# Head outputs of a tile pair split over two PSUM banks by parity, and a last feed-forward step in two halves

## The chip, the cores and the metric

The kernel runs on one core of one Trainium2 chip, in float32 (matrix products of the feed-forward layers in fp32r with each operand split into a high and a low part). The metric is the device time of one execution in microseconds. Before the change three executions took 596.48, 597.11 and 599.32 us: median 597.11.

## The reference

A chunked linear attention ("scan"), whose output goes through two feed-forward layers. Sizes: batch 4, 8 heads, sequence 768, head size 32, state size 16; 3072 tokens of 256 features; hidden size 2048.

```python
for c in range(nc):                                   # per head, chunk of the sequence
    cum = np.cumsum(la, axis=-1)
    M = CB * exp(cum_i - cum_j) * causal              # CB = C_i . B_j
    y = M @ xc + (Cc @ state) * exp(cum)              # inside the chunk + carried state
    state = exp(sum(la)) * state + sum_j B_j x_j decay_from_j
x = y as (3072 tokens, 256)                           # head h gives features 32h..32h+31
h = x @ w_in;   x = np.maximum(0.01 * h, h) @ w_out   # layer 0
h = x @ w_in2;  out = (h * np.cos(h)) @ w_out2        # layer 1
```

## The kernel before

The 768 positions are cut into six blocks of 128, and a block of all four sequences (`NB`) is 4 x 128 = 512 tokens. Per block there is an attention stage and then layer 0 and layer 1; `JOBS` orders the twelve layer jobs (0 0 0 1 1 0 1 0 1 0 1 1), and the attention of block b + 1 runs beside layer 0 of block b.

Attention works on token tiles of 128 positions of one sequence (`TokenTile`, j = 0 to 3), each in two chunks s of 64. Per tile TensorE runs `cb` (scores, L467), `products` (L487: decayed scores times x for each head and chunk; L491: the state's contribution), and `carried` (L500: state times C). All are small matmuls on parts of the array: L467, L487 and L491 on 64 rows and 32 columns, L500 on 32 rows and 32 columns. The program writes each as one float32 matmul. VectorE multiplies scores by decays (`decay`, L475) and carries the state (L524). The outputs of head h = 2p + q stand on partitions 32p to 32p + 31, in columns 256 + 64q on, and `y_cols` says so. An even tile uses the tile `att` (two PSUM banks, one for each chunk s), an odd tile two one-bank tiles of tag `g`; `x_hi` (L511, ScalarE) and `x_lo` (L515, VectorE) copy them out as the high and low parts of the layer's input x1, one instruction each for an even tile, two for an odd one. Layer 1 uses the `g` banks for hidden tiles when no attention runs.

A layer job has 16 steps f of 128 hidden features: six input matmuls (L658 to L660) into `h` (or, in layer 1, for odd f, `g`), an activation chain (layer 0: L668; layer 1: L671 ScalarE, L674 VectorE, L679 ScalarE, L683 VectorE), a split into `hi` (L306 or L308) and `lo` (L314 or L316), and six output matmuls (L698 to L700) into two `y` banks. At the end of layer 1 the two `y` are copied (L754) and stored (L757). Layer 0 of block 0 runs its first three steps in halves of 256 tokens. Weights arrive as float64 bits and are rebuilt on ScalarE, VectorE and GpSimd (L306 to L359) during the first 120 us.

The order on each engine is written out ahead of time: `Order.run` is a list scheduler that takes each operation's engine costs (us), due time, reads and writes, and starts the ready operation with the earliest due time on each free engine. An operation can hold many instructions (all `carried` of a pair and the following `cb` are one). Between engines the instructions wait on semaphores. Until the first feed-forward matmul, spare warm-up matmuls (L265) fill free TensorE time; the first `WARM_FIRST` stand at the very start.

```python
def y_cols(self, h, s):
    p, q = divmod(h, 2)
    return bank(self.t, s)[32 * p:32 * p + 32, 256 + Q * q:256 + Q * q + Q]
```

## Time and profile before

| | |
|---|---|
| median of three executions | 597.11 us (596.48 to 599.32) |
| profiled execution | 598.55 us, of which span 596.7 us (first to last instruction) |
| TensorE matmul, weight load | 98%, 80% of the span busy; 5013 instructions each |
| VectorE, ScalarE, GpSimd | 55%, 59%, 46% busy |
| mean granted TensorE clock | 0.989 |
| chain that ended last | TensorE 94%, VectorE 2%, ScalarE 2%, issue 1%, DMA 1% |
| instruction queue q8 | 39 packets, 0.64 MB |

The span runs from the first to the last instruction. Engines work side by side, so an engine's busy time is of use only where that engine sets the pace. "Issue" stands for time in which an engine waited for nothing that the profile shows. A float32 matmul shows as two records of an instruction. In an ordered list, `[x <-Y]` says that the engine was idle for x us before the instruction and that Y ended it; equal neighbours are merged into one row with their count. The last number of a table of stretches' clock column is the share of full speed granted to TensorE.

### The profile page before, as it was taken

Reading aid. Unit: us, or ns where it says so; the run is one execution under the profiler, and the core shown is the slowest. Engines: PE = TensorE matmul, PEld = TensorE weight load, DVE = VectorE, ACT = ScalarE, POOL = GpSimd, SP = SyncE. Lnnn points to the kernel's source line nnn. Section 1 sums busy time; section 2 is a strip of 40 time slices with the busy share of each in tenths; the row PEclk is TensorE's granted clock in tenths of the full one; section 3 lists DMA queues with packets and bytes.
Section 4 is the critical chain, followed back from the end, with each engine's and each line's share of the span. In section 5 each row is a group of like instructions: output and inputs, shape, how many; then the busy total and the mean of one; then the engine's idle time right before and its main releaser. Section 6 shows DMA issues by size and latency. Waiting matters only on the chain.

```text
span 596.7 us, 12418 instructions
## 1 busy us (share of the span) xinstructions
PE 584.7 (98%) x5013; PEld 475.5 (80%) x5013; DVE 326.3 (55%) x615; ACT 350.7 (59%) x575; POOL 273.6 (46%) x231
## 2 busy tenths in 40 slices
PE   6899999999999999999999999999999999999996
PEld 4688878788788888888788888878888888888884
DVE  4789996684695665661273653120665002566654
ACT  3799957679766556555335554434755444655553
POOL 2212417449613446455445445543555444654441
PEclk9799999999999999999999999999999999999999
DMA  8597534643640001001150001000000100000101
GB/s 283 175 284 238 152 108 137 215 140 111 198 124 0 1 1 37 0 2 35 43 173 2 1 1 36 1 3 0 2 1 2 35 1 0 1 1 6 30 1 36
DMA packets 25497, 39.00 MB, mean 65 GB/s; under 512 B 2176, under 2 KB 8320, under 8 KB 25440
## 3 DMA queue, kind: packets, MB, share of 16 engines
q1 hardware_dynamic: 25440, 38.22, 20.3%
q8 instruction: 39, 0.64, 0.5%
q14 instruction: 18, 0.15, 0.1%
HBM read 34.96 MB, written 3.24 MB: 64 GB/s over the span
## 4 chain that ended last, share of the span: by engine, by line
PE 94%; DVE 2%; ACT 2%; issue 1%; DMA 1%; SPq 0%; DVEq 0%; ACTq 0%
PE y L698 15%; PE y L700 14%; PE y L699 14%; PE h L658 11%; PE h L659 11%; PE h L660 11%; PE g L658 4%; PE g L659 3%; PE g L660 3%; PE att L467 1%; PE g L467 1%; PE att L500 1%; PE g L500 1%; PE att L487 1%; PE g L487 1%
## 5 line engine op out<-in xcount | busy, mean ns | idle before, releaser
L314 POOL TENSOR_TENSOR lo<-u,hi 128x512 fp32r<-128x512 f32 x160 | 210.2, 1316 | 231.3 <-DVE hi L308 87.7
L668 ACT ACTIVATE u<-h 128x512 f32<-128x512 f32 (+1 forms) x99 | 58.6, 592 | 99.8 <-PE h L660 92.2
L679 ACT ACTIVATE k<-k,half_pi 128x512 f32<-128x512 f32 x96 | 69.5, 724 | 51.1 <-DVE k L674 50.6
L306 ACT ACTIVATE hi<-u 128x512 fp32r<-128x512 f32 (+1 forms) x119 | 74.4, 625 | 7.5 <-DVE u L683 2.5
L698 PE MATMUL y<-hi,wo0h 128*128 128x512 f32 (+1 forms) x198 | 78.3, 396 | 0.0
L658 PE MATMUL h<-x1h,wi0h 128*128 128x512 f32 (+1 forms) x198 | 77.2, 390 | 0.0
L659 PE MATMUL h<-x1l,wi0h 128*128 128x512 f32 (+1 forms) x198 | 76.4, 386 | 0.0
L660 PE MATMUL h<-x1h,wi0l 128*128 128x512 f32 (+1 forms) x198 | 76.4, 386 | 0.0
L700 PE MATMUL y<-lo,wo0h 128*128 128x512 f32 (+1 forms) x198 | 76.3, 385 | 0.0
L699 PE MATMUL y<-hi,wo0l 128*128 128x512 f32 (+1 forms) x198 | 76.2, 385 | 0.0
L698 PE MATMUL y<-hi,wo1h 128*128 128x512 f32 x192 | 74.9, 390 | 0.4 <-ACT hi L306 0.4
L700 PE MATMUL y<-lo,wo1h 128*128 128x512 f32 x192 | 75.0, 390 | 0.3 <-DVE lo L316 0.3
L699 PE MATMUL y<-hi,wo1l 128*128 128x512 f32 x192 | 74.8, 389 | 0.0
L674 DVE SCALAR_TENSOR_TENSOR k<-k,h 128x512 f32<-128x512 int32 x48 | 33.0, 688 | 71.4 <-ACT k L671 71.4
L683 DVE TENSOR_TENSOR u<-h,k 128x512 f32<-128x512 f32 x48 | 33.2, 692 | 37.1 <-ACT k L679 36.3
L683 DVE TENSOR_TENSOR u<-g,k 128x512 f32<-128x512 f32 x48 | 33.2, 692 | 34.3 <-ACT k L679 32.2
L671 ACT ACTIVATE k<-h 128x512 int32<-128x512 f32 x48 | 28.6, 597 | 30.3 <-PE h L660 30.1
L671 ACT ACTIVATE k<-g 128x512 int32<-128x512 f32 x48 | 28.7, 598 | 28.3 <-PE g L660 28.2
L698 PEld LDWEIGHTS y<-hi,wo0h 128*128 128x128 f32 x198 | 37.5, 189 | 9.5 <-issue 1.4
L658 PEld LDWEIGHTS h<-x1h,wi0h 128*128 128x128 f32 x198 | 37.6, 190 | 7.8
L700 PEld LDWEIGHTS y<-lo,wo0h 128*128 128x128 f32 x198 | 37.5, 189 | 7.8 <-DVE lo L316 0.4
L660 PEld LDWEIGHTS h<-x1h,wi0l 128*128 128x128 f32 x198 | 37.6, 190 | 7.6 <-DVE wi0l L316 0.2
(129 smaller groups left out, 1055.6 us busy)
## 6 DMA issues: line engine op xcount, KB each, us to landing
raw<-w_in SPq DMA_DIRECT2D x16, 512.0 KB, 3.8
head<-headp SPq DMA_DIRECT2D x24, 256.0 KB, 4.0
tok<-tokp SPq DMA_DIRECT2D x24, 256.0 KB, 4.1
abc<-a_clip SPq DMA_DIRECT2D x40, 128.0 KB, 3.9
raw<-w_out SPq DMA_DIRECT2D x8, 512.0 KB, 3.8
out_t<-u SPq DMA_DIRECT2D x12, 256.0 KB, 2.6
x2h<-w_out SPq DMA_DIRECT2D x4, 512.0 KB, 5.1
x2l<-w_out SPq DMA_DIRECT2D x4, 512.0 KB, 4.7
```

The source lines that it names most:

```text
L306: A.activation(out, in_, AF.Copy, scale=scale, bias=bias)
L314: G.tensor_tensor(out=out, in0=a, in1=b, op=op)
L658: PE.matmul(o, lhsT=wh, rhs=xh, start=(c == 0), stop=False)
L659: PE.matmul(o, lhsT=wh, rhs=xl, start=False, stop=False)
L660: PE.matmul(o, lhsT=wl, rhs=xh, start=False, stop=(c == 1))
L668: A.activation(make(u, "u", [128, n], F32)[:, 0:m], tiles[h][:, 0:m], AF.Prelu, alpha=0.01)
L671: A.activation(make(k, "k", [128, n], I32), tiles[h], AF.Copy, scale=INV2PI, bias=0.25)
L679: A.activation(t, t, AF.Sin, bias=half_pi)
L683: V.tensor_tensor(out=t, in0=tiles[h], in1=tiles[k].bitcast(F32), op=ALU.mult)
L698: PE.matmul(o, lhsT=wh, rhs=gh, start=(f == q.start == 0), stop=False, **skip)
L699: PE.matmul(o, lhsT=wl, rhs=gh, start=False, stop=False, **skip)
L700: PE.matmul(o, lhsT=wh, rhs=gl, start=False, stop=(f == KF - 1), **skip)
```

## The change

The heads are set in two lists: `OUT_HEADS[0]` = 0, 2, 4, 6 and `OUT_HEADS[1]` = 5, 7, 1, 3. Place u of list q goes to partitions 32u on. The outputs of both tiles of a pair (j = 0, 1 or 2, 3) stand together: list 0 in the even tile's two banks, list 1 in the odd tile's two; the columns are chosen by the parity of j. The features of x1 are so permuted, and `w_in`'s rows are permuted on the host to match. `products` and `carried` run over q, chunk and place in the new order; `out_of` copies the outputs of a pair (three instructions on ScalarE, three on VectorE) as one planned operation each. Block 0 works in pairs too, and its scores use 64 columns of the array at a time instead of 32. The warm-up matmuls are 512 wide instead of 256, and half as many.

In the last job the last step f = 15 runs in two halves of 256 tokens; the second half's hidden tile has the other tag. For f > 8 of that job the output matmuls are due 3.5 steps after the input matmuls instead of 2.5. Each `y` is copied in halves (first half on ScalarE, second on VectorE) and stored in halves.

```diff
-WARM = 300
-WARM_N = 256
-WARM_FIRST = 22
+WARM = 150
+WARM_N = 512
+WARM_FIRST = 11
+OUT_HEADS = [[2 * p for p in range(4)], [2 * ((p + 2) % 4) + 1 for p in range(4)]]
...
+            w = 64 if self.first else 32
             for r in range(2):
                 for g in range(2):
-                    for c in range(4):
-                        rows, i = slice(64 * g, 64 * g + 64), Q * (c // 2)
-                        PE.matmul(bank(t, g)[32 * c:32 * c + 32, 128 * r:128 * r + 128].rearrange("p (q i) -> p q i", q=2),
-                                  lhsT=k[rows, T * r + 32 * c:T * r + 32 * c + 32],
+                    for c in range(0, T, w):
+                        rows, i = slice(64 * g, 64 * g + 64), Q * (c // Q)
+                        PE.matmul(bank(t, g)[c:c + w, 128 * r:128 * r + 128].rearrange("p (q i) -> p q i", q=2),
+                                  lhsT=k[rows, T * r + c:T * r + c + w],
                                   rhs=k[rows, 2 * T:4 * T].rearrange("p (q i) -> p q i", q=2)[:, :, i:i + Q],
                                   start=(r == 0), stop=True, skip_group_check=True)
...
-        def y_cols(self, h, s):
-            p, q = divmod(h, 2)
-            return bank(self.t, s)[32 * p:32 * p + 32, 256 + Q * q:256 + Q * q + Q]
+        def y_cols(self, q, u, s):
+            c = 256 + Q * (self.j % 2)
+            return bank(self.t - self.t % 2 + q, s)[32 * u:32 * u + 32, c:c + Q]
         def products(self):
             k, m = tiles[self.tok], tiles[self.ab]
             for q in range(2):
+                for s in range(2):
+                    for u, h in enumerate(OUT_HEADS[q]):
+                        rows = slice(Q * s, Q * s + Q)
+                        PE.matmul(self.y_cols(q, u, s), lhsT=k[rows, 32 * h:32 * h + 32], rhs=m[rows, h, :],
+                                  start=False, stop=self.first and s == 0, skip_group_check=True)
+            for s in range(2):
                 for p in range(4):
-                    for s in range(2):
-                        h, rows = 2 * p + q, slice(Q * s, Q * s + Q)
-                        PE.matmul(self.y_cols(h, s), lhsT=k[rows, 32 * h:32 * h + 32], rhs=m[rows, h, :],
-                                  start=False, stop=self.first and s == 0, skip_group_check=True)
-            for p in range(4):
-                for s in range(2):
                     PE.matmul(bank(self.t, s)[32 * p:32 * p + 32, 384:448], lhsT=k[Q * s:Q * s + Q, 256 + 32 * p:288 + 32 * p],
                               rhs=k[Q * s:Q * s + Q, 64 * p:64 * p + 64], start=False, stop=True, skip_group_check=True)
@@ -495,16 +500,17 @@
             k = tiles[self.head][:, 2 * T:4 * T].rearrange("p (q i) -> p q i", q=2)
             for s in range(self.s0, 2):
                 for q in range(2):
-                    for p in range(4):
-                        r = 32 * p
-                        PE.matmul(self.y_cols(2 * p + q, s), lhsT=tiles[self.st[s]][r:r + 32, 32 * q:32 * q + 32],
+                    for u, h in enumerate(OUT_HEADS[q]):
+                        r = 32 * (h // 2)
+                        PE.matmul(self.y_cols(q, u, s), lhsT=tiles[self.st[s]][r:r + 32, 32 * q:32 * q + 32],
                                   rhs=k[r:r + 32, q, Q * s:Q * s + Q], start=False, stop=True, skip_group_check=True)
         def out_of(self, p):
-            for o, g in banks(self.t):
-                yield (o[:, :, 256:384].rearrange("p s (q i) -> p s q i", q=2),
-                       tiles[f"x1{p}{self.b}"][:, :, T * self.j:T * self.j + T].rearrange("p q (s i) -> p s q i", s=2)[:, g])
+            x = tiles[f"x1{p}{self.b}"][:, :, T * self.j:T * self.j + 2 * T].rearrange("p q (j s i) -> p q s j i", j=2, s=2)
+            for q in range(2):
+                for o, s in banks(self.t + q):
+                    yield o[:, :, 256:384].rearrange("p s (j i) -> p s j i", j=2), x[:, q, s]
         def x_hi(self, e):
             for y, x in self.out_of("h"):
...
         def outputs(self):
-            att, b, j, slack = self.att, self.b, self.j, self.slack
-            odd = [n + "/y" for n in att_names(self.t)]
-            od.add(None, {"A": 0.36 if j % 2 else 0.28}, self.x_hi, reads=odd + [f"x1h{b}/fresh", f"x1l{b}/fresh"],
-                   writes=[f"x1h{b}/{j}"], slack=slack)
-            od.add(None, {"V": 0.42 if j % 2 else 0.34}, self.x_lo, reads=odd + [f"x1h{b}/{j}"], writes=[f"x1l{b}/{j}"], slack=slack)
+            b, j, slack = self.b, self.j, self.slack
+            y = [n + "/y" for i in range(2) for n in att_names(self.t + i)]
+            od.add(None, {"A": 0.8}, self.x_hi, reads=y + [f"x1h{b}/fresh", f"x1l{b}/fresh"],
+                   writes=[f"x1h{b}/{j}", f"x1h{b}/{j + 1}"], slack=slack)
+            od.add(None, {"V": 0.8}, self.x_lo, reads=y + [f"x1h{b}/{j}", f"x1h{b}/{j + 1}"],
+                   writes=[f"x1l{b}/{j}", f"x1l{b}/{j + 1}"], slack=slack)
...
+        def scores(group, cost, steps=(), reads=(), writes=()):
             new = [(n, "g") for x in group if x.j == 1 for n in att_names(x.t)]
-            on_pe(cost + 0.43 * len(group), group or others, [x.carried for x in others] + [x.cb for x in group],
-                  [k for x in others for k in (x.head + "/c", *x.st[x.s0:2])] + keys(others, "/y") +
-                  [x.head + k for x in group for k in ("/b", "/c")] + ([] if first else [f"run{b - 1}"]) +
-                  keys([x for x in group if x.j > 1 or (b and x.j == 0)], "/y"),
-                  keys(others, "/y") + keys(group, "/cb") + [n + "/y" for n, _ in new], new)
+            on_pe(cost, group, [*steps, *(x.cb for x in group)],
+                  [*reads, *(x.head + k for x in group for k in ("/b", "/c")), *([] if first else [f"run{b - 1}"]),
+                   *keys([x for x in group if x.j > 1 or (b and x.j == 0)], "/y")],
+                  [*writes, *keys(group, "/cb"), *(n + "/y" for n, _ in new)], new)
+        def carried(pair, group, cost):
+            return cost, [x.carried for x in group], [k for x in group for k in (x.head + "/c", *x.st[x.s0:2])] + keys(pair, "/y"), keys(pair, "/y")
...
+        for i in (0, 2):
             pair, after = tt[i:i + 2], tt[i + 2:]
             for x in pair:
                 x.prepare()
-            if not i:
-                add_cb(pair, [], 0.35)
+                if first:
+                    scores([x], 0.6)
+            if not first and not i:
+                scores(pair, 1.2)
             for x in pair:
                 x.decays()
-            on_pe(1.1, pair, [x.products for x in pair], [k for x in pair for k in (x.tok + "/b", x.tok + "/x", x.ab)],
-                  keys(pair, "/s", "/y"))
+            for group in [[x] for x in pair] if first else [pair]:
+                on_pe(0.3 + 0.36 * len(group), group, [x.products for x in group],
+                      [k for x in group for k in (x.tok + "/b", x.tok + "/x", x.ab)] + keys(pair, "/cb"), keys(group, "/s") + keys(pair, "/y"))
             for x in pair:
                 x.carries()
-            for x in after:
-                attention_loads(x.t, x.slack)
-            add_cb(after, pair, 1.0 if after else 0.85)
-            for x in pair:
-                x.outputs()
+            if first:
+                for x in pair:
+                    cost, steps, *keys_of = carried(pair, [x], 0.3)
+                    on_pe(cost, [x], steps, *keys_of)
+            else:
+                for x in after:
+                    attention_loads(x.t, x.slack)
+                if after:
+                    scores(after, *carried(pair, pair, 1.85))
+                else:
+                    cost, steps, *keys_of = carried(pair, pair, 0.85)
+                    on_pe(cost, pair, steps, *keys_of)
+            pair[0].outputs()
...
+        if tail:
+            f, _, at = steps.pop()
+            steps += [(f, q, at + i * HALF_STEP) for i, q in enumerate(half)]
         for f, q, at in steps:
             m = q.stop - q.start
             sc = m / 512.0
-            h_tag = "g" if l and f % 2 else "h"
+            h_tag = "g" if l and (f + bool(q.start)) % 2 else "h"
...
-                od.add(at + 2.5 * step, {"P": 0.681 * sc}, lambda e, c=c, mm_out=mm_out: mm_out(e, c),
+                od.add(at + (3.5 if tail and f > 8 else 2.5) * step, {"P": 0.681 * sc}, lambda e, c=c, mm_out=mm_out: mm_out(e, c),
...
+                def copy(e, q, c=c, o=o):
+                    t = tiles[o] if q.start else make(o, "u", [128, n], F32)
+                    (A.copy if e == "A" else V.tensor_copy)(t[:, q], tiles[ys[c]][:, q])
+                def store(e, q, c=c, o=o):
+                    jj = slice(q.start // T, q.stop // T)
+                    SP.dma_start(out=out.rearrange("m (j i) -> m j i", j=NB)[128 * c:128 * c + 128, jj, T * b:T * b + T],
+                                 in_=tiles[o][:, q].rearrange("p (j i) -> p j i", i=T))
+                if tail:
+                    for i, q in enumerate(half):
+                        od.add(at, {"V": 0.4} if i else {"A": 0.35}, lambda e, q=q, copy=copy: copy(e, q),
+                               reads=[ys[c]] + ([f"{o}/0"] if i else []), writes=[f"{o}/{i}"], make=[] if i else [(o, "u")])
+                        od.add(at - 20, {"S": 0.45}, lambda e, q=q, store=store: store(e, q), reads=[f"{o}/{i}"], writes=[f"{o}/out{i}"], lag=1.6)
+                    continue
...
-        "w_in": np.ascontiguousarray(moe_w_in.reshape(H // 2, 2, D, DFF).swapaxes(0, 1)).view(np.int64).reshape(DM, DFF),
+        "w_in": np.ascontiguousarray(moe_w_in.reshape(H, D, DFF)[sum(OUT_HEADS, [])]).view(np.int64).reshape(DM, DFF),
```

## Rows read from the trace of the kernel before

**Rows 1.** the page: busy us of each engine, share, instructions

```profile
PE 584.7 (98%) x5013; PEld 475.5 (80%) x5013; DVE 326.3 (55%) x615; ACT 350.7 (59%) x575; POOL 273.6 (46%) x231
```

**Rows 2.** what TensorE waited for: us in total, times, longest us

```profile
PE att L467 <- issue: 3.0, 1, 3.0
PE g L500 <- DVE st L524: 1.5, 1, 1.5
PE y L698 <- ACT hi L306: 0.4, 1, 0.4
```

**Rows 3.** stretches: us; busy (x) PE, PEld, DVE, ACT, POOL; clock, DMA, GB/s

```profile
0.00:12.30 12.30, 10.04 (x222) 6.50 (x222) 7.15 (x16) 4.42 (x6) 2.97 (x11) 1.00 0.75 260
15.30:21.00 5.70, 5.69 (x82) 3.29 (x83) 3.53 (x10) 2.17 (x6) 1.27 (x1) 0.51 0.49 163
31.00:588.00 557.00, 557.00 (x4538) 456.73 (x4538) 303.23 (x561) 331.77 (x541) 265.81 (x215) 1.00 0.18 56
588.00:592.50 4.50, 3.74 (x13) 1.83 (x11) 2.21 (x4) 1.94 (x3) 0.00 (x0) 1.00 0.01 2
```

**Rows 4.** TensorE in order of time, stage 1: start us, us, what

```profile
64.86 0.65 PE L500 MATMUL att<-head,st 32*32 32x64 f32 x32
65.33 0.62 PE L500 MATMUL g<-head,st 32*32 32x64 f32 x32
...
72.65 0.45 PE L487 MATMUL att<-abc,tok 64*32 64x64 f32 x32
72.92 0.46 PE L491 MATMUL att<-tok 64*32 64x64 f32 x16
```

**Rows 5.** the border to block 1 in order of time

```profile
77.84 0.48 DVE L515 TENSOR_TENSOR x1l<-g,x1h 128x128 fp32r<-128x128 f32 x2
...
78.52 0.39 PE L659 MATMUL h<-x1l,wi0h 128*128 128x512 f32 x1
```

**Rows 6.** TensorE in order of time at the start: the hole

```profile
11.90 0.42 PE L467 MATMUL att<-head 64*32 64x128 f32 x9
15.31 1.08 PE L467 MATMUL att<-head 64*32 64x128 f32 x23 [2.99 <-issue]
```

**Rows 7.** DMA queues, 12.3 to 13.1 us: packets, MB, share of 16 engines

```profile
q1 hardware_dynamic: 171, 0.31, 103.9%
q8 instruction: 1, 0.02, 8.5%
```

**Rows 8.** VectorE and ScalarE in order of time at the start

```profile
10.11 0.73 DVE L475 TENSOR_TENSOR abc<-g,abc 128x256 f32<-128x256 f32 x2
...
16.76 0.38 ACT L511 ACTIVATE x1h<-att 128x256 fp32r<-128x256 f32 x1 [3.87 <-DVE st L524]
...
19.84 0.45 ACT L511 ACTIVATE x1h<-g 128x128 fp32r<-128x128 f32 x2 [1.52 <-PE g L467]
```

**Rows 9.** the tail in order of time

```profile
586.42 0.39 PE L660 MATMUL g<-raw,wi1l 128*128 128x512 f32 x1
...
586.91 0.60 ACT L671 ACTIVATE k<-g 128x512 int32<-128x512 f32 x1 [0.64 <-PE g L660]
...
590.46 0.69 DVE L316 TENSOR_TENSOR lo<-u,hi 128x512 fp32r<-128x512 f32 x1 [0.76 <-ACT hi L306]
...
592.01 0.40 PE L700 MATMUL y<-lo,wo1h 128*128 128x512 f32 x1
592.36 0.53 SPq L757 DMA_DIRECT2D out_t<-u  x1
592.52 0.69 DVE L754 COPY u<-y 128x512 f32<-128x512 f32 x1 [1.36 <-PE y L700]
```

**Rows 10.** the page's DMA issues: KB each, median us to landing

```profile
out_t<-u SPq DMA_DIRECT2D x12, 256.0 KB, 2.6
```

**Rows 11.** 256-column instructions, 20 to 57 us: count, busy us, mean ns, idle

```profile
L668 ACT ACTIVATE u<-h 128x256 f32<-128x256 f32 x6 | 2.4, 408 | 0.7 <-PE h L660 0.7
L316 DVE TENSOR_TENSOR lo<-u,hi 128x256 fp32r<-128x256 f32 x6 | 2.9, 478 | 0.2
```

More of the change, by code (lines that the diff above doesn't have):

```diff
@@ L571, in keys, with on_pe @@
             return [n + k for x in group for k in kinds for n in (att_names(x.t) if k == "/y" else [x.att])]
-        def on_pe(cost, now, then, reads, writes, make=()):
+        def on_pe(cost, group, steps, reads, writes, make=()):
             def go(e):
-                for f in then:
+                for f in steps:
                     f()
-            od.add(None, {"P": cost}, go, reads=reads, writes=writes, make=make, slack=min(x.slack for x in now))
-        def add_cb(group, others, cost):
+            od.add(None, {"P": cost}, go, reads=reads, writes=writes, make=make, slack=min(x.slack for x in group))
@@ L589, in attention @@
+        def carried(pair, group, cost):
+            return cost, [x.carried for x in group], [k for x in group for k in (x.head + "/c", *x.st[x.s0:2])] + keys(pair, "/y"), keys(pair, "/y")
         for x in tt if first else tt[:2]:
             attention_loads(x.t, x.slack)
-        if first:
-            for x in tt:
-                x.prepare()
-                add_cb([x], [], 0.15)
-                x.decays()
-                on_pe(0.45, [x], [x.products], [x.tok + "/b", x.tok + "/x", x.ab], keys([x], "/s", "/y"))
-                x.carries()
-                on_pe(0.3, [x], [x.carried], [x.head + "/c", x.st[1]] + keys([x], "/y"), keys([x], "/y"))
-                x.outputs()
@@ L600, in attention @@
-        for i in () if first else (0, 2):
+        for i in (0, 2):
             pair, after = tt[i:i + 2], tt[i + 2:]
@@ L696, in mm_out @@
                 gh, gl = (tiles[v][:, 0:m] for v in (g, r))
-                skip = dict(skip_group_check=True) if l == b == 0 else {}
+                skip = dict(skip_group_check=True) if l == b == 0 or tail else {}
                 PE.matmul(o, lhsT=wh, rhs=gh, start=(f == q.start == 0), stop=False, **skip)
@@ L750, in layer @@
                 o = f"o{b}.{c}"
-                def copy(e, c=c, o=o):
-                    t = make(o, "u", [128, n], F32)
-                    (A.copy if e == "A" else V.tensor_copy)(t, tiles[ys[c]])
-                def store(e, c=c, o=o):
-                    SP.dma_start(out=out.rearrange("m (j i) -> m j i", j=NB)[128 * c:128 * c + 128, :, T * b:T * b + T],
-                                 in_=tiles[o].rearrange("p (j i) -> p j i", j=NB))
-                od.add(at, {"A": on_psum_a, "V": on_v} if c == 0 else {"V": on_v, "A": on_psum_a}, copy,
+                def copy(e, q, c=c, o=o):
[11 more added lines that the diff above has]
+                    continue
+                q = slice(0, n)
+                od.add(at, {"A": on_psum_a, "V": on_v} if c == 0 else {"V": on_v, "A": on_psum_a}, lambda e, q=q, copy=copy: copy(e, q),
                        reads=[ys[c]], writes=[o], make=[(o, "u")])
-                od.add(at - 20, {"S": 0.8 * sc}, store, reads=[o], writes=[f"{o}/out"], lag=1.6)
+                od.add(at - 20, {"S": 0.8}, lambda e, q=q, store=store: store(e, q), reads=[o], writes=[f"{o}/out"], lag=1.6)
     jobs, done = [], [0, 0]
```

18 lines of the change are left out of this document (9 added, 9 removed).

## The prediction

> **What bounds the kernel now.** I read the busy shares of the page first, then the list of what TensorE waited for, then a table by stretch. TensorE is busy 98% of the span and the next engine 59% [rows 1]. Its waits are few: one of 3.0 us near the start, for which the trace names no producer, one of 1.5, and tenths of a microsecond elsewhere [rows 2]. By stretch it is plain where it can be shortened: from 31 to 588 us TensorE is busy for all of 557.00 us [rows 3], so there time falls only where its own instructions take less. Before that lies a start whose 3.0 us hole is followed by half clock (0.51 from 15.3 to 21.0 us), and after it comes a tail in which TensorE is busy 3.74 of 4.50 us and the outputs leave. So the sum has a start, a saturated middle and a tail. No other engine enters the middle unless a new wait makes it.
>
> **The change part by part.**
>
> *Outputs by parity of head, the carried products (L500).* In the kernel before, the outputs of both parities of a pair of heads have the same 32 output partitions and the same bank, and the heads of parity 0 and 1 use the same 32x32 position of the array: eight heads on four positions, one after the other. OUT_HEADS shifts the odd heads by two partition groups and puts them into the other tile's banks, so that one sweep (q = 0, then q = 1) uses eight positions. The rows price this. A float32 matmul of the program shows as two records (16 in the code, x32 in the row). L500 for the first tile of a pair starts at 64.86 and that for the second at 65.33: 0.47 us for 32 records, 14.7 ns each; L487, which already alternates between eight positions (two row halves by four column groups), starts 32 records in 0.27 us (72.65 to the start of L491 at 72.92), 8.4 ns each [rows 4]. Per position that is 4 x 14.7 = 59 ns and 8 x 8.4 = 67 ns, so I read both as bound by the position, not by issue. A pair has 64 records. At L487's pace they take 64 x 8.4 = 0.54 us in place of 64 x 14.7 = 0.94 us: 0.40 us a pair. The bound on the other side is L491: it too alternates between eight positions, and its x16 lasts 0.46 us, as long as the 0.45 us of L487's x32 [rows 4], so a record takes about twice 8.4 ns: no gain at all. L491 comes after 32 others have run off quickly, so the second half of a pair may be slow. I take 0.35 us, near L487's end, because the first half certainly comes in the same manner (after long feed-forward matmuls). Attention stages 1 to 5 have two pairs each, all inside the saturated middle: 10 x 0.35 = -3.5 us; ends 0 and -4.0.
>
> *The order of the products (L487, L491).* Sixteen and eight matmuls as before, still eight positions, now columns first and then row halves: 0, with +1.0 and -1.0 (0.1 us for each of ten pairs) as ends, since no row shows that order.
>
> *Paired outputs.* Before: one instruction for an even tile, two for an odd one, on ScalarE and again on VectorE. After: three for the pair, the same shapes, so 0 busy time. But they come as one step, after both tiles, and the planner books 0.8 + 0.8 us one after the other. At the borders of the blocks this is close: the last x1l copies of stage 1 run from 77.84 to 78.32 us and the feed-forward matmul that reads them starts at 78.52 [rows 5]. The cover is the backlog of output matmuls (2.5 steps of the layer) that the planner can put between. I book +0.2 us in all; without that cover it would be up to 0.7 us at each of five borders, +3.5.
>
> *Start: fewer TensorE instructions.* Block 0 takes 64-wide score matmuls, so each tile needs 16 records, not 32; warm-up matmuls are twice as wide and half as many. The hole at 12.3 us sits inside one tile's score matmuls: nine records at 11.90 us, the other 23 from 15.31 us, with an idle time for which nothing is named [rows 6]. Nothing in the rows sets the tenth record apart from the ninth, and just there one packet of the instruction queue moves, among data packets that take 103.9% of the DMA time [rows 7]. I read it as TensorE out of code: it had started 222 matmul records by then [rows 3]. (The 39 packets of that queue over the span, in the table above, go well with 10,026 matmul and weight-load records: about 257 each.) After the change the same place in the work lies about 16 warm-ups, 32 score records of tiles 0 and 1 and five of tile 2 earlier in the code, at record 170. The 52 records that this frees are what remains of tile 2's scores (12), two spreads and a few warm-ups (about 8), tile 1's carried products (16) and tile 3's scores (16): they reach to the first feed-forward matmul, and by then the packet has long come. What waited is on the path: the ScalarE x1h copy sat idle 3.87 us, and the next x1h 1.52 us for score matmuls that ran at half clock [rows 8]. So -3.0 us for the hole is the first term. Against it: tile 0's products now write the banks in which tile 1's decay multiplication reads its scores (0.73 us for its two instructions [rows 8]); I add 0.6 us for the one behind the other, and 0.4 us for the even tile's x1h copy (0.38 us [rows 8]), which no longer runs early. -3.0 + 0.6 + 0.4 = -2.0. Ends: +1.0 if the hole stays as it is, and -4.9 if also the half clock of 15.3 to 21.0 us goes (5.69 us of TensorE work at 0.51 [rows 3] would be 2.9 us).
>
> The Trainium skill ("Runtime: NRT & Kernel Launch", Instruction fetch mechanics) gives blocks of 256 instructions, which agrees with the packets, but a store of 2048 instructions for TensorE and a fetch that is mostly hidden. By that the hole at about 450 instructions would not be missing code, and the start term would lose its -3.0; the unnamed wait with its one code packet speaks against it.
>
> *Tail.* The last step's six input matmuls end at 586.81 us; a chain of six operations, three on ScalarE and three on VectorE by turns, then lasts to 591.15, its first 0.60 and its last 0.69 us long; four output matmuls follow, the last from 592.01 to 592.41; the copy takes 0.69 us from 592.52 and the store 2.6 us from an issue of 0.53 [rows 9, 10]. In halves, operations on 256 columns take 0.41 us on ScalarE and 0.48 us on VectorE [rows 11]. For the second half's chain that is 3 x 0.41 + 3 x 0.48 = 2.67 in place of 3 x 0.60 + 3 x 0.69 = 3.87 us: -1.2; but VectorE does each of its three operations twice, and the first half is in front: 3 x (2 x 0.48 - 0.69) = +0.8. What follows the low part is four matmuls of half the width: from 591.21 to 592.41 is 1.20 us, half of it -0.6. Copy 0.69 to 0.48: -0.2. Four stores in place of two: the last two are issued behind each other, +0.3 of an issue of 0.53, and their landing, with half the bytes, -0.1 of 2.6. The later due time of the output matmuls (3.5 steps for 2.5) keeps matmuls for the gaps; it helps reach these numbers, and I book -0.5 for TensorE's idle 0.76 us [rows 3]. Sum: -1.2 + 0.8 - 0.6 - 0.2 + 0.3 - 0.1 - 0.5 = -1.5. Ends: -0.2 (the shared engines take the gain back) and -2.6 (no push-back on VectorE, stores apart).
>
> *Sum.* -3.5 + 0 + 0.2 - 2.0 - 1.5 = -6.8 us. The profiled execution took 598.55 us (span 596.7 and 1.85 around it), 1.4 us over the median of 597.11; from it the sum gives 591.8, from the median 590.3 us. The runs agree better with the median, so I forecast 590.3.
>
> **The rivals.**
>
> *The start keeps its hole*: it moves to another instruction, or it is not missing code. For it: the DMA engines are full until after the hole, so a packet asked for later may also come later. Against: the 52 records of reserve. Start term 0 in place of -2.0: 592.3 us. The page of the Trainium skill named above would give this time.
>
> *The carried products stay at 15 ns a record*, as L491 does, so that a position more brings nothing; that is also the case in which the change does not do what it says. 0 in place of -3.5: 593.8 us.
>
> *Shared banks make new waits, and it gets slower.* With both tiles of a pair in the same banks, each matmul group on them waits for ScalarE and VectorE to leave them. For it: an x1h copy waited for PE L467, a group that writes other columns of the same tile [rows 8]. Against: groups in the middle have two to ten microseconds between them, and the planner fills these with feed-forward matmuls. The place is the products of a second pair, behind three x1h and three x1l copies of the first, on every pair; if a wait of 1.5 us (the 1.52 of [rows 8]) stays uncovered on ten pairs it costs 15 us: 590.3 + 15 = 605.3 us. It decides from 0.7 us a pair (6.8 / 10), and counts as slower from 1.0.
>
> The Trainium skill ("PSUM — Partial Sum Buffer", PSUM bank collisions raise a hardware error) says to guard by bank and quarter of the partitions, not by address, which is the reason for such waits; that wait of the trace agrees with it.
>
> **How the numbers follow.** Forecast 0.62, hole stays 0.20, carried products no faster 0.13, new waits 0.05. 0.5% is 3.0 us, about what a measurement of this kernel can tell from no change, so faster means under 594.1 and slower over 600.1. Faster: 0.60 of the forecast's 0.62, 0.18 of 0.20, 0.09 of 0.13: 0.87. Slower: 0.04 of the new waits and 0.01 of a failed start: 0.05. The rest 0.08. The range goes from 585.8, with the lower ends of the carried products, the start and the tail together (-4.0 - 4.9 - 2.6 + 0.2 = -11.3), to 595.0, where the first two rivals hold both, one of them for all but 0.6 us (-1.5 - 0.6 = -2.1); the forecast's own range is 588 to 592.
>
> **What would show it.** L500's records for a pair in 0.55 us, not 0.94. In the list of TensorE's waits the unnamed 3.0 us gone or under 1 us, and the first feed-forward matmul at 18 to 19.5 us, not 21.1. No wait over 0.3 us between 31 us and the tail. From the end of the last input matmul to the end of the span 8.4 us in place of 9.9. The forecast is wrong if the hole comes back behind record 222 with the same length, if the pace of L500 stays, or if TensorE waits at block borders for x1l or at products for a bank.

## The result, and the profile after

The changed kernel took 590.87 us (median of four, 589.60 to 594.77), the kernel before 597.81 us (median of four, 596.48 to 599.32): ratio 0.9897 [0.9854, 0.9939]. The forecast was 590.3. The profiled execution of the changed kernel is the slowest of its four, 594.77 us with a span of 592.8; some 3.6 us of it, by an estimate from its rows (1.93 us of standstill and half of 3.4 us at half clock), are a stall that two further profiled executions don't have (below). So a second profiled execution stands beside it where it matters, 589.28 us with a span of 587.4, called "the repeat".

The page of the changed kernel, to be set against [rows 1] (busy us, share, instructions):

```profile
PE 579.5 (98%) x4941; PEld 469.5 (79%) x4941; DVE 326.2 (55%) x615; ACT 352.3 (59%) x582; POOL 270.6 (46%) x232
```

TensorE has 72 matmul records fewer and is busy 5.2 us less; the other engines do what they did. What it waited for, the answer to [rows 2], first in the changed kernel, then in the repeat:

```profile
PE att L471 <- issue: 1.9, 1, 1.9
PE h L672 <- ACT u L682: 1.4, 3, 0.7
PE att L505 <- DVE st L530: 1.3, 1, 1.3
...
PE h L672 <- DVE tok L279: 1.1, 1, 1.1
...
PE att L505 <- issue: 0.7, 1, 0.7
```

```profile
PE h L672 <- ACT u L682: 1.0, 3, 0.6
PE att L505 <- DVE st L530: 1.1, 1, 1.1
PE h L672 <- DVE tok L279: 1.0, 1, 1.0
PE att L505 <- issue: 0.2, 1, 0.2
```

(L672 to L674 are the input matmuls, L713 to L715 the output matmuls, L471 the scores, L492 and L496 the products, L505 the carried products, L266 the warm-ups; before they were L658 to L660, L698 to L700, L467, L487 and L491, L500, L265. On the other engines L517 and L521 copy x1h and x1l, L530 carries the state, L435 is a scan that prepares its decays, L307, L315 and L317 make high and low parts, L682 is the activation of layer 0; before they were L511, L515, L524, L432, L306, L314, L316, L668.) The 3.0 us without a producer are gone, but "issue" has not gone: it stands at other places, in smaller pieces. New are also three waits of the input matmuls for the activation (L682), 1.4 and 1.0 us in all; they lie between 22 and 29 us. The stretches show the rest (the columns of [rows 3]), first the changed kernel, then the repeat:

```profile
15.90:17.50 1.60, 0.48 (x3) 0.03 (x1) 1.60 (x7) 1.60 (x3) 0.89 (x1) 1.00 0.93 301
31.00:152.50 121.50, 120.19 (x1584) 96.95 (x1583) 95.59 (x186) 99.16 (x160) 57.09 (x52) 1.00 0.55 169
152.50:159.00 6.50, 4.57 (x74) 3.36 (x72) 2.92 (x10) 3.06 (x7) 2.70 (x4) 0.74 0.87 247
```

```profile
31.00:152.50 121.50, 120.39 (x1635) 96.86 (x1634) 96.79 (x186) 98.88 (x161) 57.32 (x54) 1.00 0.54 172
152.50:159.00 6.50, 6.50 (x119) 4.97 (x118) 6.50 (x15) 4.99 (x8) 2.65 (x3) 1.00 0.63 230
```

From 159 us to the tail TensorE is busy throughout. The middle is saturated as before but for one wait of 1.1 to 1.3 us before 152 us, and the granted clock, 0.51 for 5.7 us at the start before [rows 3], is 1.00 there now. Between 152.5 and 159 us the two executions part: the changed kernel's profile loses 1.93 us of TensorE time (6.50 - 4.57) and runs at a mean clock of 0.74, the repeat loses nothing.

### The profile page after: what moved, and what is told of

It reads as the page before. It is cut to its first block, busy times and chain, and to the rows that moved or that the text cites. A ratio compares the mean times of both kernels' runs of the same rounds, so it can differ in the third digit from the quotient of the medians.

```text
span 592.8 us, 12291 instructions
## 1 busy us (share of the span) xinstructions
PE 579.5 (98%) x4941; PEld 469.5 (79%) x4941; DVE 326.2 (55%) x615; ACT 352.3 (59%) x582; POOL 270.6 (46%) x232
## 4 chain that ended last, share of the span: by engine, by line
PE 94%; DVE 2%; ACT 1%; DMA 1%; issue 1%; SPq 0%; DVEq 0%; ACTq 0%
PE y L713 15%; PE y L714 15%; PE y L715 15%; PE h L672 12%; PE h L673 11%; PE h L674 11%; PE g L674 4%; PE g L673 4%; PE g L672 4%; PE att L471 1%; PE g L471 1%; PE att L505 1%; DMA head<-headp 1%; PE att L492 1%; PE g L505 1%
## 5 line engine op out<-in xcount | busy, mean ns | idle before, releaser
L315 POOL TENSOR_TENSOR lo<-u,hi 128x512 fp32r<-128x512 f32 (+1 forms) x159 | 207.7, 1309 | 226.9 <-DVE hi L309 92.2
L682 ACT ACTIVATE u<-h 128x512 f32<-128x512 f32 (+1 forms) x99 | 58.7, 594 | 87.2 <-PE h L674 79.7
L694 ACT ACTIVATE k<-k,half_pi 128x512 f32<-128x512 f32 (+1 forms) x97 | 69.8, 720 | 49.0 <-DVE k L689 48.3
L672 PE MATMUL h<-x1h,wi0h 128*128 128x512 f32 (+1 forms) x198 | 79.4, 401 | 2.5 <-ACT u L682 1.4
L307 ACT ACTIVATE hi<-u 128x512 fp32r<-128x512 f32 (+1 forms) x123 | 76.3, 620 | 7.6 <-DVE u L698 2.6
L713 PE MATMUL y<-hi,wo0h 128*128 128x512 f32 (+1 forms) x198 | 76.5, 387 | 0.0
L674 PE MATMUL h<-x1h,wi0l 128*128 128x512 f32 (+1 forms) x198 | 76.1, 384 | 0.0
L715 PE MATMUL y<-lo,wo0h 128*128 128x512 f32 (+1 forms) x198 | 75.8, 383 | 0.0
L713 PE MATMUL y<-hi,wo1h 128*128 128x512 f32 (+1 forms) x194 | 75.1, 387 | 0.0
L714 PE MATMUL y<-hi,wo1l 128*128 128x512 f32 (+1 forms) x194 | 75.1, 387 | 0.0
L715 PE MATMUL y<-lo,wo1h 128*128 128x512 f32 (+1 forms) x194 | 75.0, 387 | 0.0
L689 DVE SCALAR_TENSOR_TENSOR k<-k,h 128x512 f32<-128x512 int32 (+1 forms) x49 | 33.4, 682 | 71.8 <-ACT k L685 71.8
L698 DVE TENSOR_TENSOR u<-h,k 128x512 f32<-128x512 f32 (+1 forms) x49 | 33.6, 686 | 37.1 <-ACT k L694 37.0
L698 DVE TENSOR_TENSOR u<-g,k 128x512 f32<-128x512 f32 (+1 forms) x48 | 32.9, 686 | 33.1 <-ACT k L694 31.3
L672 PEld LDWEIGHTS h<-x1h,wi0h 128*128 128x128 f32 x198 | 37.4, 189 | 13.5 <-ACT u L682 2.0
L685 ACT ACTIVATE k<-h 128x512 int32<-128x512 f32 (+1 forms) x49 | 29.1, 593 | 30.3 <-PE h L674 30.3
L685 ACT ACTIVATE k<-g 128x512 int32<-128x512 f32 (+1 forms) x48 | 28.6, 595 | 27.4 <-PE g L674 27.2
L674 PEld LDWEIGHTS h<-x1h,wi0l 128*128 128x128 f32 x198 | 37.5, 189 | 7.6
L713 PEld LDWEIGHTS y<-hi,wo0h 128*128 128x128 f32 x198 | 37.2, 188 | 7.8
L715 PEld LDWEIGHTS y<-lo,wo0h 128*128 128x128 f32 x198 | 37.2, 188 | 7.4
```

The source lines that it names most:

```text
L307: A.activation(out, in_, AF.Copy, scale=scale, bias=bias)
L315: G.tensor_tensor(out=out, in0=a, in1=b, op=op)
L672: PE.matmul(o, lhsT=wh, rhs=xh, start=(c == 0), stop=False)
L674: PE.matmul(o, lhsT=wl, rhs=xh, start=False, stop=(c == 1))
L682: A.activation(make(u, "u", [128, n], F32)[:, 0:m], tiles[h][:, 0:m], AF.Prelu, alpha=0.01)
L685: A.activation(make(k, "k", [128, n], I32)[:, 0:m], tiles[h][:, 0:m], AF.Copy, scale=INV2PI, bias=0.25)
```

## The experiments

Times are medians; each ratio is to the kernel before, run beside it on the same chip.

**Where the code runs out.** In the kernel before, TensorE stopped inside tile 2's scores [rows 6]. My reading (missing code) says that the stop belongs to a count of instructions; the alternative, that it belongs to that place in the work. So I kept the kernel before and only filled it with smaller warm-ups, so that the same count falls on other work:

```diff
-WARM = 300
-WARM_N = 256
-WARM_FIRST = 22
+WARM = 600
+WARM_N = 128
+WARM_FIRST = 44
```

> The kernel before with warm-up matmuls of 128 columns instead of 256 and twice as many, so that the same places of the work lie later in the code. Theory (the hole is missing code, one block of it after another): TensorE stops again at its 222nd matmul record, which is now in the products of tile 1 (about 52 + 4 + 6 warm-ups in front), and further stops without a producer lie multiples of about 125 to 128 records behind. Rival (the hole belongs to a place in the work, such as tile 2's head data or a semaphore): TensorE stops again after the ninth score record of tile 2, which is then about record 255.

One run: 596.95 us beside 598.97, no difference that one run can carry. But the stop moved. TensorE in order of time:

```profile
11.43 0.39 PE L491 MATMUL g<-tok 64*32 64x64 f32 x9
13.40 0.31 PE L491 MATMUL g<-tok 64*32 64x64 f32 x7 [1.58 <-issue]
```

It now stands in tile 1's state product, not in tile 2's scores, and again nothing sets the tenth record apart from the ninth. Up to there it is 222 matmuls, as many as before [rows 3]:

```profile
0.00:12.50 12.50, 10.63 (x222) 8.70 (x223) 7.23 (x16) 4.91 (x6) 2.96 (x10) 1.00 0.78 268
```

Counted over all the TensorE instruction records of the trace (matmuls, weight loads and a few others), the stop stands behind number 449 here, in the kernel before, in all three profiles of the changed kernel and in four of the experiments below (start alone, without its start, carried products, tail). In three more (order of the products, the first with 64-wide scores, fewer warm-ups) it stands behind 446 to 448, and these traces lack one to three matmul records in front of it. In the thirteenth trace the packet came early (below). The changed kernel's first profile has two more stops, behind 705 and behind 4033: 449 + 256 and 449 + 14 x 256. This experiment has a second one too, 0.69 us at 105.44 us, behind 3009 = 449 + 10 x 256, and the next experiment one of 0.79 us at 104.68 us, behind 2753 = 449 + 9 x 256. And each time TensorE goes on 1.2 to 1.6 us after a packet of the instruction queue has landed: packet 12.06, start 13.40 here (103.99 and 105.44 for the second); 14.02 and 15.31 in the kernel before; 15.99 and 17.50 in the changed kernel; 15.28 and 16.68 in the repeat. With the count, the packet and the delay the same while the work differs, I take it as shown that the stop is missing code.

The Trainium skill ("Runtime: NRT & Kernel Launch", Instruction fetch mechanics) has code coming in blocks of 256 instructions, and the distances 256 and 14 x 256 agree. Its store of 2048 instructions for TensorE and its fetch that is mostly hidden do not fit a stop behind the 449th that lasts up to 3.0 us; the measurement decides.

**The start alone.** The kernel before with the change's warm-ups and 64-wide scores in block 0, nothing else:

```diff
-WARM = 300
-WARM_N = 256
-WARM_FIRST = 22
+WARM = 150
+WARM_N = 512
+WARM_FIRST = 11
...
+            w = 64 if self.first else 32
...
-                    for c in range(4):
+                    for c in range(0, T, w):
```

> The kernel before with only the smaller code at the start: 512-wide warm-up matmuls, half as many, and 64-wide scores in block 0; no pairing, no parity, old tail. TensorE's code ran out after 449 of its instruction records in every trace so far. Theory (less code lets more work be done before that place): the stop is again at record 449, now behind tile 1's carried products or tile 3's scores, and the first feed-forward matmul comes 2.5 to 4 us earlier than in the kernel before: 594 to 595.5. Rival (the smaller code pays only together with the pairing, which had put work in front): the stop moves, but the first feed-forward matmul stays within 1 us of 21.1, and so does the time.

596.04 us beside 598.24, ratio 0.9959 [0.9945, 0.9973]: -2.2 us, about the size that I had booked. But the stop is there. TensorE in order of time (one line more ahead of them: L488 are products here, L659 is the first input matmul):

```profile
15.06 0.30 PE L488 MATMUL att<-abc,tok 64*32 64x64 f32 x5
16.39 0.56 PE L488 MATMUL att<-abc,tok 64*32 64x64 f32 x22 [1.03 <-issue]
...
19.00 0.78 PE L659 MATMUL h<-x1h,wi0h 128*128 128x256 f32 x1
```

Wider warm-ups and scores put more time into the same number of instructions, so TensorE reaches number 449 at 15.36 us instead of 12.32, 3.0 us later, while the packet comes 1.0 us later (14.98 for 14.02). Hence the stop is 2.0 us shorter, 1.03 for 2.99, and the first feed-forward matmul starts at 19.00 instead of 21.10. The gain is a stop made shorter, not one taken away.

**The change without its start.** The changed kernel with the old warm-ups (300, 256, 22) and `w = 32` everywhere.

> The changed kernel with the 256-wide warm-up matmuls and 32-wide scores in block 0, that is with the old amount of TensorE code at the start. Theory (the hole at 12.3 us is missing code): a stop of 2 to 3 us for which nothing is named comes back at about the 222nd matmul record, the first feed-forward matmul comes at 20 to 21 us instead of 17.5, and the time rises by 2 to 3 us, to about 593. Rival (the pairing of the first block's tiles moved the start): first feed-forward matmul and time as in the changed kernel.

597.33 us beside 598.19, ratio 0.9992 [0.9974, 1.0010]: without its start the change gains nothing that can be told, though its three other parts are in it. TensorE in order of time:

```profile
12.88 0.29 PE L505 MATMUL att<-head,st 32*32 32x64 f32 x3
14.39 0.25 PE L505 MATMUL att<-head,st 32*32 32x64 f32 x3 [1.22 <-issue]
...
16.03 1.25 PE L471 MATMUL g<-head 64*32 64x128 f32 x32 [0.71 <-ACT x1h L517]
17.21 2.32 PE L266 MATMUL h<-hi 128*128 128x256 bf16 x10
```

The stop now falls into tile 0's carried products, ahead of everything that block 0's outputs hang on; TensorE then waits 0.71 us for the paired x1h copies and fills up with warm-ups at half clock (0.50 from 17 to 19 us), and the first feed-forward matmul starts at 20.17 us. But a good part of the loss lies later. From 31 to 580 us TensorE is idle for 3.5 us, and for 1.1 us in the repeat. The longest wait there is 2.2 us for the low part of a weight. TensorE, VectorE and GpSimd, each in order of time:

```profile
67.92 0.50 PE L674 MATMUL h<-x1h,wi0l 128*128 128x512 f32 x1 [2.19 <-DVE wi0l L317]
```

```profile
66.11 1.75 DVE L317 TENSOR_TENSOR wi0l<-k,wi0h 128x512 fp32r<-128x512 f32 x1
```

```profile
66.01 1.31 POOL L315 TENSOR_TENSOR wo0l<-k,wo0h 128x512 fp32r<-128x512 f32 x1 [3.90 <-ACT wo0h L307]
```

The VectorE instruction takes 1.75 us beside the GpSimd one, where the median of its kind is 0.68. The start is thus worth 2.2 us in the old kernel and 6.5 in the new one (597.33 - 590.82). Of the 6.7 us between the two profiled executions (594.1 - 587.4) 2.4 are idle time of TensorE behind 31 us, so that the old code at the start cannot be said to cost all of it there. Which of the waits makes the 4 us of difference was not separated.

**The carried products.** The changed kernel with the odd heads unshifted, so that both parities of a pair of heads use the same 32x32 position; banks, order and planner's costs stay.

```diff
-OUT_HEADS = [[2 * p for p in range(4)], [2 * ((p + 2) % 4) + 1 for p in range(4)]]
+OUT_HEADS = [[2 * p for p in range(4)], [2 * p + 1 for p in range(4)]]
```

> The changed kernel with the odd heads in places 1, 3, 5, 7 (not shifted): both parities still write two pairs of banks, but head 2p and 2p + 1 use the same 32x32 position again. Theory (the position sets the pace of L505): a pair's 64 records go back from about 0.59 us to 0.9 us, and the time rises by 10 x 0.35 = 3.5 us over the changed kernel, to about 594. Rival (the split into banks by parity is what made them faster): pace and time as in the changed kernel.

593.01 us beside 598.19, ratio 0.9918 [0.9896, 0.9940]; the changed kernel took 590.82 beside it, so the shift is worth 2.2 us. One pair in order of time, this kernel, then the changed one (L471 is what follows):

```profile
151.09 0.31 PE L505 MATMUL att<-head,st 32*32 32x64 f32 x8
...
151.90 0.29 PE L505 MATMUL g<-head,st 32*32 32x64 f32 x8
152.12 0.45 PE L471 MATMUL att<-head 64*32 64x128 f32 x16
```

```profile
151.69 0.26 PE L505 MATMUL att<-head,st 32*32 32x64 f32 x4
...
151.96 0.33 PE L505 MATMUL att<-head,st 32*32 32x64 f32 x5
...
152.47 0.51 PE L471 MATMUL att<-head 64*32 64x128 f32 x17
```

On the same positions a pair takes 1.03 us (151.09 to 152.12), as before. With the shift it takes 0.78: the first 32 records 0.27 us, 8.4 ns each, and the other 32 0.51 us, 16 ns each. So the shared position is what makes the first half slow; something else bounds the second, and what, was not tried. Ten pairs: 10 x (1.026 - 0.784) = 2.4 us, by the medians over the pairs of these two kernels.

**The order of the products.** The changed kernel with the loops of L492 and L496 turned back.

```diff
-                for s in range(2):
-                    for u, h in enumerate(OUT_HEADS[q]):
+                for u, h in enumerate(OUT_HEADS[q]):
+                    for s in range(2):
...
-            for s in range(2):
-                for p in range(4):
+            for p in range(4):
+                for s in range(2):
```

> The changed kernel with the products in the old order (both chunks of a head one after the other, for L492 and L496), still by parity into the two tiles' banks. A pair's products take 1.28 us before and 1.17 us in the changed kernel. Theory: the order (four columns of one row half, then of the other) makes the difference: 1.28 us again and +1.1 us. Rival: the order does nothing, and the split of the banks gives the 0.11 us a pair: 1.17 us and no change in time.

590.74 us beside 598.97, ratio 0.9872 [0.9852, 0.9892]: the order does nothing. Yet a pair's products have become shorter, here as in the changed kernel. From the first product to the next group, before and after:

```profile
153.19 0.45 PE L487 MATMUL att<-abc,tok 64*32 64x64 f32 x32
...
154.47 0.50 PE L698 MATMUL y<-hi,wo0h 128*128 128x512 f32 x1
```

```profile
65.58 0.34 PE L492 MATMUL att<-abc,tok 64*32 64x64 f32 x16
...
66.75 0.50 PE L713 MATMUL y<-hi,wo0h 128*128 128x512 f32 x1
```

1.28 us before, 1.17 after, and the median over all ten pairs is the same: -1.1 us in ten pairs. It is 1.17 us in the experiment without the shift too. What is left for it is that each tile's outputs go to two pairs of banks (`att`, `g`); this was not tried by itself.

**The tail.** The changed kernel with the last step whole, whole copies and stores, and output matmuls due after 2.5 steps.

```diff
-        if tail:
+        if False:
...
-                od.add(at + (3.5 if tail and f > 8 else 2.5) * step, ...
+                od.add(at + 2.5 * step, ...
...
-                if tail:
+                if False:
```

> The changed kernel with the last step, its copies and its stores whole again and the output matmuls due 2.5 steps later, as before. Theory: the tail is worth 1.5 us, so about 592; from the end of the last input matmul to the end of the span 9.9 us again. Rival (the engines that both halves share take the gain back): within 0.5 us of the changed kernel.

592.14 us, ratio 0.9910 [0.9883, 0.9937]; +1.3 us against the changed kernel's 590.82. The changed kernel's tail in order of time, and its stores (KB each, us to landing), to be set against [rows 9, 10]:

```profile
583.86 0.28 PE L674 MATMUL h<-raw,wi1l 128*128 128x256 f32 x1
...
586.64 0.43 DVE L317 TENSOR_TENSOR lo<-u,hi 128x256 fp32r<-128x256 f32 x1 [0.56 <-ACT hi L307]
...
588.04 0.28 PE L715 MATMUL y<-lo,wo1h 128*128 128x256 f32 x1
588.39 1.99 SPq L773 DMA_DIRECT2D out_t<-u  x4
```

```profile
out_t<-u SPq DMA_DIRECT2D x4, 128.0 KB, 1.9
```

From the start of the last input matmul to the end of the span: 10.28 us before (586.42 to 596.7), 10.28 in this experiment (583.22 to 593.5), 8.94 in the changed kernel (583.86 to 592.8) and 8.94 in the repeat (578.46 to 587.4). TensorE no longer idles between the chain's last operations: held-back output matmuls run up to 588.04 without a gap.

**The changed kernel again**, twice, for the spread and for further profiles.

> The changed kernel again, for a ratio over five rounds and a second profile. Theory (sum of start -2.0, carried products -3.5, tail -1.5): 590 to 591 us. In the first profile of the changed kernel TensorE stood still for 1.9 us at 153 us and ran at half clock from 155.4 to 158.8 us; if that belongs to the single execution (missing code while the DMA engines are full) it need not be there, or not in that place, in this profile, and the span is about 588; if it belongs to the kernel it is there again and the span is near 592.8.

> The changed kernel a third time, on the same chip as the next: 590.8, from its median of five rounds. The stop at record 4033 that three of the traces show near 153 us comes or stays away by chance of the execution.

590.82 us, ratio 0.9888 [0.9862, 0.9914] (the repeat is its profile), and 591.21, 0.9887 [0.9871, 0.9902]. The stall at 152.5 us is in neither profile. In the first one it looks so, TensorE in order of time:

```profile
152.47 0.51 PE L471 MATMUL att<-head 64*32 64x128 f32 x17
154.92 0.34 PE L471 MATMUL att<-head 64*32 64x128 f32 x8 [1.93 <-issue]
```

It is the stop behind record 4033, in the middle of one tile's scores, and then 3.4 us at half clock (a 512-wide matmul in 0.43 us instead of 0.23, from start to start). The code packet landed at 153.42 us. In the repeat, which comes to that place at about 151 us, it landed at 149.61, and there is no stop. The experiments on the tail and on the order of the products have it too. So it hangs on when the packet lands in an execution, not on a part of the change that was tried.

**Fewer instructions still.** If code supply bounds the start and the small matmuls run at some 8 to 16 ns a record, 64-wide scores in all blocks should help a little more:

```diff
-            w = 64 if self.first else 32
+            w = 64
```

> The changed kernel with 64-wide scores in all blocks, not only in block 0: 16 records a tile instead of 32, the same arithmetic. A pair's scores took 1.09 us with 32-wide pieces in blocks 1 to 5; in block 0 a tile's 16 records lasted as long as 32 did before (0.67 us). Theory: no gain in the scores themselves, but 320 fewer matmul records in the dense stretches, so the stop of 1.9 us and the half clock behind it that two of the profiles show at 153 us do not occur: 0 to -1.5 us against the changed kernel, about 590. Rival: a pair's scores get slower with four positions instead of eight, +0.3 us a pair, 593.

> 64-wide scores in all blocks, beside the changed kernel on one chip. Its scores took 1.03 us a pair instead of 1.09 (0.5 us in ten pairs), and its trace has no stop near 153 us. Theory: 0.5 to 1.5 us under the changed kernel, 589.3 to 590.3. Rival (the difference of the first comparison was between chips): the same as the changed kernel within 0.3 us.

589.32 us, ratio 0.9841 [0.9825, 0.9856]; again, beside the changed kernel on one chip, 590.02, 0.9865 [0.9850, 0.9880], to its 591.21 and 0.9887. It beats both kernels, the changed one by about 1.2 us. The scores of a pair take 1.03 us instead of 1.09, 0.5 us in ten pairs; the rest was not traced. In the second of these profiles the first code packet happened to land at 13.92 us, before TensorE came to its place, and there is no stop. TensorE in order of time:

```profile
15.18 1.04 PE L266 MATMUL h<-hi 128*128 128x512 bf16 x4
15.88 0.45 PE L672 MATMUL h<-x1h,wi0h 128*128 128x256 f32 x1
```

Then at most 18 warm-ups as well, to save more code (with the limit of 150 the changed kernel places 23):

> As the one with 64-wide scores in all blocks, and at most 18 warm-up matmuls instead of the 23 that are placed in the changed kernel, so that the first feed-forward matmul lies before record 222. In the changed kernel it is record 222 itself. Theory (it waits for code, not for VectorE as the wait is put down): it starts 0.5 to 1.0 us earlier, when x1l and wi0l are there, and the time is 589.5. Rival (it waits for the data): it starts as before, at 16.7 us or later, and the time is that of the 64-wide kernel; with the clock at half in front of it, 591 or more.

590.38 us, ratio 0.9858 [0.9842, 0.9873]: not better. The planner put attention in front instead, the stop fell into tile 2's products, 0.83 us, the first feed-forward matmul came at 19.93, and the clock stood at half from 14.4 to 24.6 us. The clock had fallen before the stop began. Whether it fell for want of warm-ups or by the new order was not separated.

## Why the prediction was right, and where it was not

The time was right (590.87 for 590.3), and the parts seem to add up to it: carried products -2.4 and products -1.1 by their records, tail -1.3, start -2.2 in the kernel before, together -7.0, for -6.8 booked and -6.9 measured. That it fits so well is partly luck. The 1.1 us booked too much for the carried products and the 1.1 us that the products gained unpriced cancel, and taken out of the changed kernel the start is worth 6.5 us, not 2.2, so the parts aren't independent and their sum proves little.

**Carried products, -3.5: mechanism right, size off.** They measured -2.4. The step that failed is the 0.35 us a pair: I took L487's pace for nearly the whole pair. The first half has it (8.4 ns), the second has 16 ns, as L491's row had warned [rows 4]. Half a pair at each pace gives 32 x 8.4 + 32 x 16 ns = 0.78 us, a gain of 0.25 on the 1.03 us measured before.

**Order of the products, 0: right for the order** (590.74 with the old one); but the same instructions gained 1.1 us, which I had not priced at all; that the split of banks gives it is left over, not shown.

**Paired outputs, +0.2: right in the middle of the kernel, wrong at the start.** No input matmul waits for an x1h or x1l copy at a border between blocks. In block 0 with the old code TensorE waits 0.71 us for the paired x1h copies.

**Start, -2.0: the claim wrong, the size met by luck.** I wrote that the place would move 52 records, to the first feed-forward matmul, "and by then the packet has long come". The place did move exactly there: record 449 is the last one ahead of the first L672. The packet had not come. The start of the repeat in order of time:

```profile
14.76 1.29 POOL L315 TENSOR_TENSOR wi0l<-k,wi0h 128x512 fp32r<-128x512 f32 x1
...
15.18 0.48 DVE L521 TENSOR_TENSOR x1l<-g,x1h 128x128 fp32r<-128x128 f32 x2
...
16.65 0.19 PEld L672 LDWEIGHTS h<-x1h,wi0h 128*128 128x128 f32 x1 [1.50 <-issue]
16.68 0.36 PE L672 MATMUL h<-x1h,wi0h 128*128 128x256 f32 x1 [1.04 <-DVE tok L279]
...
16.99 0.28 PE L674 MATMUL h<-x1h,wi0l 128*128 128x256 f32 x1
```

The low part of the input is there at 15.66 and that of the weight, the last to come, at 16.05; L674, which needs it, starts at 16.99. The profile puts L672's wait down to a VectorE instruction that it doesn't read (L279 writes `tok`); the weight load just ahead says "issue", and the code packet landed at 15.28. In three other experiments the profile puts the wait at this place down to L479 or L355, which write other tiles again. So the stop still costs 0.9 us here (16.99 - 16.05), and 1.0 us in the changed kernel's profile, by the same two instructions (17.81 - 16.79). The start gained because the stop is shorter and stands behind more work: first L672 at 16.7 to 17.7 us instead of 21.1. Some of that is lost again to the waits for L682 between 22 and 29 us, 1.0 to 1.4 us, which I had not foreseen. The half clock that I had put into the lower end of this term (-4.9) is gone too: the clock is 1.00 from 12 to 26 us. So the step that failed is the -3.0 for the hole, booked whole: it shrank from 2.99 to 1.0 us, so about 2 us of it came, and the half clock, left out of the sum, went besides. The 0.6 and 0.4 us set against it were not measured by themselves. The rival "the start keeps its hole" was right about the hole, to which I had given one chance in five, and wrong about its price.

**Tail, -1.5: right**, -1.34 in the trace and -1.3 in the time. From the end of the last input matmul to the end of the span it is 8.66 us, where I forecast 8.4. The single terms of this sum were not measured one by one.

**New waits.** The rival of shared banks did not come: no wait of TensorE for a bank on every pair. "No wait over 0.3 us between 31 us and the tail" was wrong: apart from the stop at 152.5 us, the carried products wait 1.1 to 1.3 us for the state (L530), up to 69.54 us in the repeat and up to 71.08 in the changed kernel's first profile. The third profile has 0.99 us of it, and 0.43 more at 160.55. VectorE, then GpSimd, in the repeat in order of time:

```profile
65.97 3.00 DVE L435 TENSOR_TENSOR_SCAN tok<-tok,ident 128x64 f32<-128x64 f32 x4
...
69.22 0.27 DVE L530 SCALAR_TENSOR_TENSOR st<-st,tok,att 128x64 f32<-128x64 f32 x1
```

```profile
65.46 3.01 POOL L315 TENSOR_TENSOR lo<-u,hi 128x512 fp32r<-128x512 f32 x2
```

Four scans took 3.00 us where the median of all 44 is 0.266 us each. Two of them are the long ones, 1.39 and 1.33 us; each began while a GpSimd instruction ran and ended 0.15 us after it. The other two came when both were over and took 0.26 us each. The Trainium skill ("SBUF — State Buffer", SBUF: two separate sides) says that a VectorE instruction with two inputs in SBUF and a GpSimd one that reads SBUF lock each other out for a whole instruction; the rows agree. That this overlap, and not the paired step itself, is the cause of TensorE's wait was not tested.

## What to carry to other kernels

A stall without a producer in the middle of a run of equal instructions is worth a count: if it comes back behind the same number of instructions with other work there, and each time soon after a packet of the instruction queue, it is code supply, and fewer, larger instructions ahead of it make it shorter. It doesn't go because the place moves: ask when the packet lands and what the DMA engines carry then. Small matmuls that share a position of the array can be spread over more positions, but price the second half of a group from the slow row, not from the fast one. Parts of a change that sum up to its time are no proof of the parts: take each out of the changed kernel, and see where in the trace the time comes back.

## What the runs showed of the hardware

- Code for TensorE ran out behind instruction 449 in twelve of thirteen traces (three of them counted with their missing records), and in some behind others a multiple of 256 further on: 0.2 to 3.0 us of idle time each, ending 1.2 to 1.6 us after the packet landed. A stop can show as a wait for a producer whose data the instruction doesn't read.
- 32x32 matmuls: 14.7 ns a record with eight on four positions; with eight positions 8.4 ns for the first 32 records and 16 ns for the next.
- The clock fell to 0.5 inside or after stops of 3.0, 1.93, 1.2 and 1.0 us (kernel before, 152.5 us in the changed one, old start in the new kernel, new start in the old one), but stayed at 1.00 through the 1.1 us of the changed kernel's start, and through 1.51 us at 155 us with the old order of the products. The length of the stop alone does not decide it.
- Two scans that began beside a GpSimd instruction took 1.39 and 1.33 us, where the median is 0.266; a VectorE subtraction took 1.75 us beside one, where the median is 0.68.
- Four stores of 128 KB landed in 1.9 us each, where those of 256 KB take 2.6 [rows 10].
